# Gated linear attention and a maxout layer in one kernel: w2 by halves, weight loads interleaved, and a gate on the first token group

## The chip, the cores and the metric

The kernel runs on one core of one Trainium2 chip. The metric is the device time of one execution in microseconds. A core has TensorE (PE, matrix products), VectorE (DVE), ScalarE (ACT), GpSimd (POOL) and SyncE (SP), which here issues every DMA. Each engine works through its own list of instructions in order and waits for others on semaphores. Matmul results land in PSUM accumulators, which ScalarE or VectorE must empty.

## The reference

```python
B, H, S, D = 4, 8, 768, 48
for t in range(S):                       # attention with a decaying state
    state = alpha[:, :, t, :, None] * state + k[:, :, t] (outer) v[:, :, t]
    y[:, :, t] = q[:, :, t] @ state
x = y.transpose(0, 2, 1, 3).reshape(3072, 384)
out = maximum(x @ w1, x @ w2) @ w_out    # d_ff = 1024
```

All inputs and the output are fp32 in HBM: q, k, v and alpha 4.7 MB each, each weight 1.57 MB, the output 4.7 MB.

## The kernel before

**Attention in chunks.** The sequences are cut into 24 chunks of 128 tokens. Batch 0 is done in three double chunks of 256 tokens (functions d1, dcs, dexp, dqk, dtp, dp, dkv, dy; names with d), the other 18 chunks singly (a1, p1, a2, p2, p3, p4). A chunk takes the logarithm of alpha (ScalarE, dloga), sums it along time by matmuls with constant masks (TensorE, tile dcs or cs), makes exp of plus and minus the sum (ScalarE, den and dep), multiplies k and q by them (GpSimd dkt, VectorE dqt), transposes both (TensorE, dtp or tp), copies them out (dqk), forms the scores (TensorE, dpa and dpb), masks them (VectorE, dpt), and sums scores and the carried state into y (TensorE, dy or y). ScalarE copies y, transposed, into xT as fp16. The state passes from chunk to chunk through dkv, dw, dg, dt and dT.

**The maxout layer.** It uses max(x w1, x w2) = x w2 + relu(x (w1 - w2)). So wd = w1 - w2 is made once on VectorE in two halves (prep_wd, L657), M = w2 w_out is made once on TensorE, and the output is x M + relu(x wd) w_out. For M, w2 is cast to fp16 (copy, L653), transposed by 24 TensorE transposes (prep_t, L663, tile wtp), copied to w2T (prep_te), and multiplied with the cast w_out (prep_m, L677, tile mp; three blocks of 128 rows, each two calls of four matmuls). Tokens are then taken in groups of one to three chunks: eight h steps (fstep, L688, three matmuls each, as wide as the group) with a relu each (L693 on VectorE, L695 on ScalarE), and for each chunk an output tile in two halves (tstep: three matmuls with M at L702 and three of relu at L705; then five more at L705), a copy (outs) and a store (L715). h, y, mp and op share three PSUM accumulators.

**What sets the order.** A planner written in the kernel (Sched, L50) holds a list of operations with costs, dependencies and priorities, walks through them in planned time and emits each where the plan puts it. So the plan decides the order in each engine's list once, when the program is built; on the chip the engines follow that order whatever the real times are. The function refill (L939) adds token groups to the plan when TensorE would fall idle, from those chunks whose xT is planned to be done; a group takes fewer than three chunks only if TensorE would otherwise idle. The numbers in the op calls are planned costs.

**The opening.** All loads go through SP's one queue in this order: the first double chunk (alpha, k, q in two halves, and v), w2 whole (L221), w_out in two halves (L231), w1 in two halves (L221), the second and third double chunks (L201), then the single chunks (L192), whose buffers are slices of the weights' fp32 tiles, free once the casts and wd are done. Meanwhile the engines work through double chunk 0, the casts, the transposes, M, wd, and the first token groups.

```python
lw2 = prev = op("w2", 0, {"SP": WLOAD}, lambda e: load_w2(), ...)
for kind in ("wo", "w1"):
    for i in range(2):
        ...
w2c = [op("w2c", s, c, ... copy(e, w216[:, s, :], w2f[:, s, :]), deps=[lw2], prio=0.6) ...]
```

Of the kernel before, what the change touches and what calls it, by code (L numbers as in the profile page):

```python
# [49 lines left out]
class Sched:  # L50
# [49 lines left out]
    def run(self):  # L100
        while True:
            c = self.pick("PE")
            if c and self.refill:
                self.refill(c[1], c[1] > self.free["PE"] + 0.3)
            best = None
            for e in self.todo:
                c = self.pick(e)
                if c and (best is None or c[1] < best[0]):
                    best = (c[1], e, c[2])
            if best is None:  # L110
                if self.refill and self.refill(1e9, True):
# [24 lines left out]
def kernel(  # L136
# [27 lines left out]
    ND = NCH // 2  # L164
# [562 lines left out]
    def op(*a, **k):  # L727
        return Op(S, *a, **k)
# [41 lines left out]
    dloads_of(2, 0.6)  # L770

    w2c = [
        op("w2c", s, c, lambda e, s=s: copy(e, w216[:, s, :], w2f[:, s, :]), deps=[lw2], prio=0.6)
        for s, c in enumerate(({"ACT": 0.95}, {"DVE": 0.65}, {"ACT": 0.95, "DVE": 0.65}))
    ]
    wdc = [[op("wd", i, {"DVE": 1.7}, lambda e, i=i: prep_wd(i), deps=[lw1[i], lw2], prio=0.6)] for i in range(2)]
    woc = [op("woc", f, {"ACT": 0.75, "DVE": 0.55},
              lambda e, f=f: copy(e, wo16[:, f : f + 2, :], wof[:, f : f + 2, :]), deps=[lwo[f // 4]])
           for f in range(0, NF, 2)]
    for n in range(2 * ND, NCG):  # L780
        loads_of(n)
        if n == 2 * ND:
            G[n]["ld", 0].after.append(prev)
        if n < 2 * ND + 6:
            for i in range(4):
                G[n]["ld", i].deps.extend(woc if n < 2 * ND + 2 else w2c + wdc[0] + wdc[1])

    w2t = []
    for f in range(0, NF, 2):
        b = Buf(rx)  # L790
        t = op("w2t", f, {"PE": 0.4}, lambda e, f=f: prep_t(f), lat=0.17, deps=w2c, alloc=[b], prio=500 + f)
        w2t.append(op("w2te", f, {"DVE": 0.6, "ACT": 0.75}, lambda e, f=f: prep_te(e, f), deps=[t], reads=[b]))
    mdone = []
    prev = None
    for s in range(3):
        b = Buf(rm)
        for i in range(2):
# [7 lines left out]
    smask = op("mask", 0, {"DVE": 1.0}, lambda e: set_mask(), prio=0.1)  # L805
# [4 lines left out]
    rdloga, rdqt, rdkt, rdv, rdT, rdw, rdt32, rdgg, rdg = (Ring(2) for _ in range(9))  # L810
    B2 = []
    for m in range(ND):
        g = GD[m]
# [9 lines left out]

        def add(name, h, engs, fn, deps, lat=0.1, alloc=(), reads=(), **kw):
            o = GD[m - 1].get((name, h)) if m else None
            g[name, h] = op("d" + name, (m, h), engs, fn, lat=lat, deps=deps, after=[o, g.get((name, h - 1))],
                            alloc=[B[x] for x in alloc], reads=[B[x] if not isinstance(x, Buf) else x for x in reads],
                            prio=2 * m + 0.3 * h, **kw)
            return g[name, h]

        for h in range(2):
            al = lambda x: [x] if h == 0 else []
            re = lambda x: [x] if h else []
            add("a1", h, {"ACT": 0.43}, lambda e, m=m, h=h: d1(m, h), [g["ld", 0, h], sp1 if m == 1 else None],
                alloc=al("loga"), reads=[L[0]] + re("loga"))
            add("p1", h, {"PE": 0.5}, lambda e, m=m, h=h: dcs(m, h), [g["a1", h]], lat=0.17, alloc=[("cs", h)], reads=["loga"])
            add("en", h, {"ACT": 0.39}, lambda e, m=m, h=h: dexp(m, h, "en", -1.0), [g["p1", h]],
                alloc=al("en"), reads=[("cs", h)] + re("en"))
            add("ep", h, {"ACT": 0.39}, lambda e, m=m, h=h: dexp(m, h, "ep", 1.0), [g["en", h]],
                alloc=al("ep"), reads=[("cs", h)] + re("ep"))  # L840
            add("gg", h, {"ACT": 0.2}, lambda e, m=m, h=h: dgg(m, h), [g["ep", h]],
                alloc=al("gg"), reads=[("cs", h)] + re("gg"))
            add("kt", h, {"POOL": 1.0}, lambda e, m=m, h=h: dqk(m, h, 1), [g["en", h], g["ld", 1, h]],
                alloc=al("kt"), reads=["en", L[1]] + re("kt"))
            add("qt", h, {"DVE": 0.7}, lambda e, m=m, h=h: dqk(m, h, 2), [g["ep", h], g["ld", 2, h]],
                alloc=al("qt"), reads=["ep", L[2]] + re("qt"))
# [4 lines left out]
            add("v2", h, {"DVE": 0.64, "ACT": 0.92}, lambda e, m=m, h=h: dtpe(e, m, h), [g["p2", h]],  # L851
                alloc=[("qk", h)], reads=[("tp", h)])
            add("p3", h, {"PE": 0.36}, lambda e, m=m, h=h: dp(m, h), [g["v2", h]], lat=0.17,
                alloc=[("pa", h), ("pb", h)], reads=[("qk", h)], tiled=True)
            for t in range(2):
                add("m" + str(t), h, {"DVE": 0.62}, lambda e, m=m, h=h, t=t: dmask(m, h, t),
                    [g["p3", h], smask, g.get(("m0", h))],
                    alloc=[] if t else [("pt", h)], reads=[(("pa", "pb")[t], h)] + ([("pt", h)] if t else []))
        add("pk", 0, {"PE": 0.38}, lambda e, m=m: dkv(m), [g["kt", 1], g["v", 1]], lat=0.17,
# [26 lines left out]
    for n in range(2 * ND, NCG):  # L886
# [7 lines left out]

        def add(name, engs, fn, deps, lat=0.1, alloc=(), reads=(), **kw):

            g[name] = op(name, n, engs, fn, lat=lat, deps=deps, after=[dep(n - 1, name) if name != "a3" or n > 2 * ND else None],
                         alloc=[B[x] for x in alloc], reads=[B[x] if isinstance(x, str) else x for x in reads],
                         prio=n, **kw)
            return g[name]  # L900
# [4 lines left out]
        add("ep", {"ACT": 0.39}, lambda e, n=n: a2(n, "ep", 1.0), [g["en"]], alloc=["ep"], reads=["cs"])  # L905
        add("gg", {"ACT": 0.2}, lambda e, n=n: a2g(n), [g["ep"]], alloc=["gg"], reads=["cs"])
# [100 lines left out]
```

## Time and profile before

| what | value |
|---|---|
| five runs, median (lowest to highest) | 149.37 us (148.66 to 149.62) |
| the profiled execution: its time, its span | 148.21 us, 146.4 us |
| TensorE busy, matmuls | 131.2 us (90%), 1982 |
| ScalarE, VectorE, GpSimd busy | 98.5, 86.4, 81.4 us |
| granted TensorE clock | 0.999 |
| moved by DMA | 28.62 MB, 195 GB/s over the span |
| h matmuls by width | 48 of 128, 48 of 256, 144 of 384 columns |
| w1 - w2, two halves on VectorE | 1.76 us each, at 19.71 and 21.80 |
| M: first and last matmul start | 17.11 us, the last group of 18 at 18.91 for 3.10 |
| w2 lands | by 12.94 us (first cast) |
| last output copy | starts at 142.91 us |

Times in the page count from the span's start. A row of the trace holds a start, a duration, the engine, the line, the tile written and the tile read, the shape, a count of like instructions in a row, and in brackets the idle time ahead of it with what ended it. A matmul's bar contains a modelled end of some 0.2 us after its last column has gone in, so bars of matmuls that follow each other overlap.

### The profile page before, as it was taken

To read this page: it belongs to the slowest core of one execution; us is meant where nothing else is said; L and a number is where in the kernel's file an instruction comes from. 1 tells how busy PE (TensorE), PEld (TensorE's weight loads), DVE (VectorE), ACT (ScalarE), POOL (GpSimd) and SP (SyncE) were. 2 spreads that over 40 slices of the span, in tenths; PEclk is the share of its full clock that TensorE was granted. 3 is DMA by queue.
4 is the path that set the end of the run, shared out by engine and by line. 5 is a ranking of instruction groups with operands and counts; after the bars stand their busy time and mean duration, and the time that the engine had idled before them with its cause. 6 is when DMAs were issued, how large, how long until landed. Compare 5 with 4: busy or idle time off the path is not lost.

```text
span 146.4 us, 4919 instructions
## 1 busy us (share of the span) xinstructions
PE 131.2 (90%) x1982; PEld 87.2 (60%) x1982; DVE 86.4 (59%) x170; ACT 98.5 (67%) x221; POOL 81.4 (56%) x182
## 2 busy tenths in 40 slices
PE   0476995889999999999999999999999999999990
PEld 0354755576777666666656666566566666556550
DVE  4666657378797589547775788675749765000000
ACT  4437856498777687699767966597577854926721
POOL 7997001659988859757775958346859670000000
PEclk9999999999999999999999999999999999999999
DMA  4999999999987999998999979798997711113022
GB/s 123 263 381 380 380 333 263 236 251 203 211 167 174 206 187 245 209 221 189 236 192 220 260 173 235 140 267 193 225 240 158 166 58 54 54 43 116 7 80 81
DMA packets 93142, 28.62 MB, mean 195 GB/s; under 512 B 87872, under 2 KB 91968, under 8 KB 93120
## 3 DMA queue, kind: packets, MB, share of 16 engines
q1 hardware_dynamic: 93120, 28.32, 80.9%
q8 instruction: 15, 0.25, 0.7%
q14 instruction: 7, 0.06, 0.1%
HBM read 23.59 MB, written 4.72 MB: 193 GB/s over the span
## 4 chain that ended last, share of the span: by engine, by line
PE 63%; SPq 16%; DMA 9%; DVE 4%; ACT 3%; issue 2%; POOL 0%; ACTq 0%; DVEq 0%
PE op L705 20%; PE h L688 17%; PE op L702 7%; SPq L201 7%; DMA dqf<-in_q_dram 6%; PE y L463 5%; SPq L192 4%; SPq L221 3%; PE pa L404 3%; DMA w1f<-in_alpha_dram 3%; PE tp L386 2%; PE tp L388 2%; PE cs L328 2%; DVE dpt L559 2%; PE kv L415 2%
## 5 line engine op out<-in xcount | busy, mean ns | idle before, releaser
L705 PE MATMUL op<-wo,g 128*128 128x384 f16 x192 | 37.8, 326 | 0.0
L688 PE MATMUL h<-xT,wd 128*128 128x384 f16 (+2 forms) x240 | 37.3, 294 | 0.5 <-DVE g L693 0.4
L688 PEld LDWEIGHTS <-wd 128*128 128x128 f16 x240 | 20.1, 97 | 10.3 <-issue 0.8
L695 ACT ACTIVATE g<-h 128x384 f16<-128x384 f32 (+2 forms) x57 | 24.1, 443 | 3.1 <-PE h L688 2.8
L705 PEld LDWEIGHTS <-g 128*128 128x128 f16 x192 | 17.7, 97 | 10.9
L653 ACT COPY qk<-tp 128x1024 f16<-128x1024 f16 x14 | 14.2, 1012 | 4.1 <-PE tp L388 3.9
L653 ACT COPY outs<-op 128x384 f32<-128x384 f32 x16 | 7.7, 479 | 12.7 <-PE op L705 12.7
L365 POOL TENSOR_TENSOR T<-w,g 48x192 f16<-48x192 f32 x30 | 15.4, 512 | 1.1
L702 PE MATMUL op<-m,xT 128*128 128x384 f16 x72 | 15.7, 326 | 0.3 <-DVE g L693 0.3
L423 DVE TENSOR_TENSOR pt<-pa,u 128x512 f16<-128x512 f32 x18 | 12.4, 688 | 4.7 <-PE pb L404 4.3
L434 DVE TENSOR_TENSOR w<-kv,t 48x192 f32<-48x192 f32 x24 | 8.5, 354 | 9.3 <-PE kv L415 8.8
L519 POOL TENSOR_TENSOR dkt<-dkf,den 128x384 f16<-128x384 f32 x6 | 5.9, 995 | 13.0 <-ACT den L501 13.0
L693 DVE TENSOR_SCALAR g<-h 128x384 f16<-128x384 f32 (+2 forms) x23 | 9.8, 437 | 4.2 <-PE h L688 4.0
L423 DVE TENSOR_TENSOR pt<-pb,u 128x512 f16<-128x512 f32 x18 | 12.2, 680 | 0.0
L467 ACT CAST xT<-y 128x384 f16<-128x384 f32 x18 | 8.6, 480 | 5.0 <-PE y L463 4.8
L350 POOL TENSOR_TENSOR kt<-w2f,en 128x384 f16<-128x384 f32 x6 | 6.3, 1056 | 5.8 <-ACT en L338 3.7
L338 ACT ACTIVATE en<-cs 128x384 f32<-128x384 f32 x18 | 9.0, 498 | 0.8 <-PE cs L332 0.5
L463 PE MATMUL y<-pt,v 128*32 128x128 f16 x288 | 9.0, 220 | 0.0
L338 ACT ACTIVATE ep<-cs 128x384 f32<-128x384 f32 x18 | 8.9, 497 | 0.0
L702 PEld LDWEIGHTS <-xT 128*128 128x128 f16 x72 | 6.3, 97 | 4.0 <-issue 0.2
L350 POOL TENSOR_TENSOR kt<-w1f,en 128x384 f16<-128x384 f32 x6 | 6.2, 1032 | 4.2 <-issue 1.7
L486 PE MATMUL dcs<-dloga,c 128*128 128x192 f16 x6 | 1.6, 268 | 7.4 <-ACT dloga L476 7.4
(121 smaller groups left out, 276.1 us busy)
## 6 DMA issues: line engine op xcount, KB each, us to landing
out_dram<-outs SPq DMA_DIRECT2D x24, 192.0 KB, 3.2
w2f<-in_moe_w_dram SPq DMA_DIRECT2D x1, 1536.0 KB, 8.2
wof<-in_moe_w_out_dram SPq DMA_DIRECT2D x2, 768.0 KB, 9.8
w1f<-in_moe_w_dram SPq DMA_DIRECT2D x2, 768.0 KB, 12.2
dvf<-in_v_dram SPq DMA_DIRECT2D x3, 384.0 KB, 5.7
wof<-in_alpha_dram SPq DMA_DIRECT2D x6, 192.0 KB, 3.8
wof<-in_k_dram SPq DMA_DIRECT2D x6, 192.0 KB, 4.8
wof<-in_q_dram SPq DMA_DIRECT2D x6, 192.0 KB, 4.4
```

Source lines behind the costliest of these rows:

```text
L201: nc.sync.dma_start(out=dloads[m][i][:, hs], in_=src[0, hs, m * C2 : (m + 1) * C2, :].rearrange("h (p j) d -> p h (j d)", j=2),)
L338: nc.scalar.activation(out=t, in_=csv, func=ACTF.Exp, scale=scale)
L350: nc.gpsimd.tensor_mul(out=kts[n % NB][:, :, 0:D], in0=loads[n][1], in1=st[n]["en"])
L365: nc.gpsimd.tensor_mul(out=st[n]["T16"][ps, :, D * t : D * t + D], in0=st[n - 1]["w"][ps], in1=st[n]["g"][ps].unsqueeze(2).to_broadcast([D ...
L423: nc.vector.tensor_mul(out=s["pt"][:, t], in0=s["pp"][t], in1=ub)
L463: nc.tensor.matmul(y[o : o + 32, b // 4, :], lhsT=lhsT, rhs=rhs, start=start, stop=stop)
L653: {"ACT": nc.scalar.copy, "DVE": nc.vector.tensor_copy, "POOL": nc.gpsimd.tensor_copy}[e](out=out, in_=in_)
L688: nc.tensor.matmul(h[:, 0:W], lhsT=wd16[:, s, f * 128 : (f + 1) * 128], rhs=xT[:, s, a : a + W], start=(s == 0), stop=(s == 2))
L693: nc.vector.tensor_relu(gts[a][:, f, 0:W], hs[a, f][:, 0:W])
L695: nc.scalar.activation(out=gts[a][:, f, 0:W], in_=hs[a, f][:, 0:W], func=ACTF.Relu)
L702: nc.tensor.matmul(op, lhsT=xT[:, s, t0 : t0 + C], rhs=m16[:, s, :], start=(s == 0), stop=False)
L705: nc.tensor.matmul(op, lhsT=gts[a][:, f, i * C : (i + 1) * C], rhs=wo16[:, f, :], start=False, stop=(f == NF - 1))
```

## The change

- w2 is loaded as two halves of 512 columns; the weight loads follow each other as w2 half 0, w2 half 1, w_out half 0, w1 half 0, w_out half 1, w1 half 1 (before: w2, w_out twice, w1 twice).
- w2 is cast in six pieces of 128x512: row block 0 on ScalarE, 1 on VectorE, 2 on GpSimd, for each half; before, three pieces of 128x1024, two of them on ScalarE and one on VectorE as built.
- The transposes of w2 wait for their half alone, and a half sum of M for its two w2T copies and two casts of w_out alone; the priorities of these and of wd are raised.
- refill makes no token group until the first half of wd is planned to be done within 0.3 us.
- The planner prices TensorE at 1.9 times the cost before 19 us of planned time, some planned costs are altered, and ep and gg are planned to follow p1 (in order behind en), not to wait for en.
- In the built program the first token group has two chunks (24 h matmuls of 256 columns); before there were two groups of one (48 of 128). The other groups have the same widths. TensorE's list begins: double chunk 0 up to the transposes of its second half, 6 transposes of w2, scores, 18 transposes, dy, the 24 matmuls of M, both dcs of double chunk 1, 9 h, dtp, 9 h, dtp, 3 h. Before: all of double chunk 0, 24 transposes, M, 6 h, dcs, 3 h, dcs, 15 h, half an output tile, dtp, the other half, dtp.

```diff
+            if e == "PE" and t < 19.0:
+                cost *= 1.9
...
-    def load_w2():
-        load_w(moe_w2, w2f, slice(0, DFF))
+    def load_w2(i):
+        load_w(moe_w2, w2f, slice(i * FH, (i + 1) * FH))
...
+    def prep_w2(e, s, i):
+        c = slice(i * FH, (i + 1) * FH)
+        copy(e, w216[:, s, c], w2f[:, s, c])
...
-    dloads_of(0, 0.0)
-    lw2 = prev = op("w2", 0, {"SP": WLOAD}, lambda e: load_w2(), lat=1.6, after=[prev], prio=0.5)
-    lw1, lwo = [], []
-    for kind in ("wo", "w1"):
-        for i in range(2):
-            fn = {"wo": load_wo, "w1": load_w1}[kind]
-            prev = op(kind, i, {"SP": WLOAD / 2}, lambda e, i=i, fn=fn: fn(i), lat=1.6, after=[prev], prio=0.5)
-            (lwo if kind == "wo" else lw1).append(prev)
-    dloads_of(1, 0.3)
-    dloads_of(2, 0.6)
+    lw2, lw1, lwo = [None] * 2, [None] * 2, [None] * 2
+    for x in "d0 w20 w21 wo0 w10 wo1 w11 d1 d2".split():
+        if x[0] == "d":
+            dloads_of(int(x[1]), 0.3 * int(x[1]))
+        else:
+            i = int(x[2])
+            fn, to = {"w2": (load_w2, lw2), "wo": (load_wo, lwo), "w1": (load_w1, lw1)}[x[:2]]
+            prev = to[i] = op(x, i, {"SP": WLOAD / 2}, lambda e, i=i, fn=fn: fn(i), lat=1.6, after=[prev], prio=0.5)
...
+    w2c = [[op("w2c", (s, i), c, lambda e, s=s, i=i: prep_w2(e, s, i), deps=[lw2[i]], prio=-0.5)
+            for s, c in enumerate(({"ACT": 0.54}, {"DVE": 0.4}, {"POOL": 0.8}))] for i in range(2)]
+    wdc = [[op("wd", i, {"DVE": 1.7}, lambda e, i=i: prep_wd(i), deps=[lw1[i], lw2[i]], prio=0.2)] for i in range(2)]
...
-        t = op("w2t", f, {"PE": 0.4}, lambda e, f=f: prep_t(f), lat=0.17, deps=w2c, alloc=[b], prio=500 + f)
+        t = op("w2t", f, {"PE": 0.4}, lambda e, f=f: prep_t(f), lat=0.17, deps=w2c[f // NFH], alloc=[b], prio=f - 10)
...
-                      deps=w2t + woc[2 * i : 2 * i + 2], after=[prev], alloc=[b] if i == 0 else (), prio=800 + s)
+                      deps=w2t[2 * i : 2 * i + 2] + woc[2 * i : 2 * i + 2], after=[prev],
+                      alloc=[b] if i == 0 else (), reads=[b] if i else (), prio=0.4 + 0.01 * s)
...
+        if wdc[0][0].done is None or wdc[0][0].done > now + 0.3:
+            return
```

More of the change, by code (lines that the diff above doesn't have):

```diff
@@ L759, in dloads_of @@
                     GD[m]["ld", i, x] = prev
-    dloads_of(0, 0.0)
-    lw2 = prev = op("w2", 0, {"SP": WLOAD}, lambda e: load_w2(), lat=1.6, after=[prev], prio=0.5)
-    lw1, lwo = [], []
-    for kind in ("wo", "w1"):
-        for i in range(2):
-            fn = {"wo": load_wo, "w1": load_w1}[kind]
-            prev = op(kind, i, {"SP": WLOAD / 2}, lambda e, i=i, fn=fn: fn(i), lat=1.6, after=[prev], prio=0.5)
-            (lwo if kind == "wo" else lw1).append(prev)
-    dloads_of(1, 0.3)
-    dloads_of(2, 0.6)
[L772 to L776, printed above, removed]
+    lw2, lw1, lwo = [None] * 2, [None] * 2, [None] * 2
[9 more added lines that the diff above has]
+    wdc = [[op("wd", i, {"DVE": 1.7}, lambda e, i=i: prep_wd(i), deps=[lw1[i], lw2[i]], prio=0.2)] for i in range(2)]
     woc = [op("woc", f, {"ACT": 0.75, "DVE": 0.55},
-              lambda e, f=f: copy(e, wo16[:, f : f + 2, :], wof[:, f : f + 2, :]), deps=[lwo[f // 4]])
+              lambda e, f=f: copy(e, wo16[:, f : f + 2, :], wof[:, f : f + 2, :]), deps=[lwo[f // 4]], prio=-0.3)
            for f in range(0, NF, 2)]
@@ L785 @@
             for i in range(4):
-                G[n]["ld", i].deps.extend(woc if n < 2 * ND + 2 else w2c + wdc[0] + wdc[1])
+                G[n]["ld", i].deps.extend(woc if n < 2 * ND + 2 else w2c[0] + w2c[1] + wdc[0] + wdc[1])
     w2t = []
@@ L790 @@
         b = Buf(rx)
-        t = op("w2t", f, {"PE": 0.4}, lambda e, f=f: prep_t(f), lat=0.17, deps=w2c, alloc=[b], prio=500 + f)
-        w2t.append(op("w2te", f, {"DVE": 0.6, "ACT": 0.75}, lambda e, f=f: prep_te(e, f), deps=[t], reads=[b]))
+        t = op("w2t", f, {"PE": 0.4}, lambda e, f=f: prep_t(f), lat=0.17, deps=w2c[f // NFH], alloc=[b], prio=f - 10)
+        w2t.append(op("w2te", f, {"DVE": 0.6, "ACT": 0.75}, lambda e, f=f: prep_te(e, f), deps=[t], reads=[b], prio=-0.4))
     mdone = []
-    prev = None
     for s in range(3):
         b = Buf(rm)
+        prev = None
         for i in range(2):
             prev = op("m", s, {"PE": 0.66}, lambda e, s=s, i=i: prep_m(s, i), lat=0.17,
-                      deps=w2t + woc[2 * i : 2 * i + 2], after=[prev], alloc=[b] if i == 0 else (), prio=800 + s)
+                      deps=w2t[2 * i : 2 * i + 2] + woc[2 * i : 2 * i + 2], after=[prev],
+                      alloc=[b] if i == 0 else (), reads=[b] if i else (), prio=0.4 + 0.01 * s)
         mdone.append(op("mev", s, {"ACT": 0.4, "DVE": 0.45}, lambda e, s=s: copy(e, m16[:, s, :], mps[s]),
@@ L804 @@
     sp1 = op("pads", 1, {"DVE": 0.5}, lambda e: set_pads(1), prio=0.9)
-    smask = op("mask", 0, {"DVE": 1.0}, lambda e: set_mask(), prio=0.1)
+    smask = op("mask", 0, {"DVE": 1.5}, lambda e: set_mask(), prio=0.1)
     sdv = [op("dvT", i, {"POOL": 0.6}, lambda e, i=i: set_dvT(i), prio=(-1, 0.9)[i]) for i in range(2)]
@@ L810 @@
     rdloga, rdqt, rdkt, rdv, rdT, rdw, rdt32, rdgg, rdg = (Ring(2) for _ in range(9))
+    AFTER = {"ep": "en", "gg": "ep"}
     B2 = []
@@ L825, in add @@
             o = GD[m - 1].get((name, h)) if m else None
-            g[name, h] = op("d" + name, (m, h), engs, fn, lat=lat, deps=deps, after=[o, g.get((name, h - 1))],
+            g[name, h] = op("d" + name, (m, h), engs, fn, lat=lat, deps=deps, after=[o, g.get((name, h - 1)), g.get((AFTER.get(name), h))],
                             alloc=[B[x] for x in alloc], reads=[B[x] if not isinstance(x, Buf) else x for x in reads],
@@ L833 @@
             re = lambda x: [x] if h else []
-            add("a1", h, {"ACT": 0.43}, lambda e, m=m, h=h: d1(m, h), [g["ld", 0, h], sp1 if m == 1 else None],
+            add("a1", h, {"ACT": 0.45}, lambda e, m=m, h=h: d1(m, h), [g["ld", 0, h], sp1 if m == 1 else None],
                 alloc=al("loga"), reads=[L[0]] + re("loga"))
             add("p1", h, {"PE": 0.5}, lambda e, m=m, h=h: dcs(m, h), [g["a1", h]], lat=0.17, alloc=[("cs", h)], reads=["loga"])
-            add("en", h, {"ACT": 0.39}, lambda e, m=m, h=h: dexp(m, h, "en", -1.0), [g["p1", h]],
+            add("en", h, {"ACT": 0.44}, lambda e, m=m, h=h: dexp(m, h, "en", -1.0), [g["p1", h]],
                 alloc=al("en"), reads=[("cs", h)] + re("en"))
-            add("ep", h, {"ACT": 0.39}, lambda e, m=m, h=h: dexp(m, h, "ep", 1.0), [g["en", h]],
+            add("ep", h, {"ACT": 0.44}, lambda e, m=m, h=h: dexp(m, h, "ep", 1.0), [g["p1", h]],
                 alloc=al("ep"), reads=[("cs", h)] + re("ep"))
-            add("gg", h, {"ACT": 0.2}, lambda e, m=m, h=h: dgg(m, h), [g["ep", h]],
+            add("gg", h, {"ACT": 0.2}, lambda e, m=m, h=h: dgg(m, h), [g["p1", h]],
                 alloc=al("gg"), reads=[("cs", h)] + re("gg"))
-            add("kt", h, {"POOL": 1.0}, lambda e, m=m, h=h: dqk(m, h, 1), [g["en", h], g["ld", 1, h]],
+            add("kt", h, {"POOL": 1.05}, lambda e, m=m, h=h: dqk(m, h, 1), [g["en", h], g["ld", 1, h]],
                 alloc=al("kt"), reads=["en", L[1]] + re("kt"))
-            add("qt", h, {"DVE": 0.7}, lambda e, m=m, h=h: dqk(m, h, 2), [g["ep", h], g["ld", 2, h]],
+            add("qt", h, {"DVE": 0.9}, lambda e, m=m, h=h: dqk(m, h, 2), [g["ep", h], g["ld", 2, h]],
                 alloc=al("qt"), reads=["ep", L[2]] + re("qt"))
@@ L850 @@
                 alloc=[("tp", h)], reads=["qt", "kt"])
-            add("v2", h, {"DVE": 0.64, "ACT": 0.92}, lambda e, m=m, h=h: dtpe(e, m, h), [g["p2", h]],
+            add("v2", h, {"DVE": 0.66, "ACT": 0.95}, lambda e, m=m, h=h: dtpe(e, m, h), [g["p2", h]],
                 alloc=[("qk", h)], reads=[("tp", h)])
@@ L855 @@
             for t in range(2):
-                add("m" + str(t), h, {"DVE": 0.62}, lambda e, m=m, h=h, t=t: dmask(m, h, t),
+                add("m" + str(t), h, {"DVE": 0.66}, lambda e, m=m, h=h, t=t: dmask(m, h, t),
                     [g["p3", h], smask, g.get(("m0", h))],
@@ L895, in add @@
         def add(name, engs, fn, deps, lat=0.1, alloc=(), reads=(), **kw):
-            g[name] = op(name, n, engs, fn, lat=lat, deps=deps, after=[dep(n - 1, name) if name != "a3" or n > 2 * ND else None],
+            g[name] = op(name, n, engs, fn, lat=lat, deps=deps, after=[g.get(AFTER.get(name)), dep(n - 1, name) if name != "a3" or n > 2 * ND else None],
                          alloc=[B[x] for x in alloc], reads=[B[x] if isinstance(x, str) else x for x in reads],
@@ L904 @@
         add("en", {"ACT": 0.39}, lambda e, n=n: a2(n, "en", -1.0), [g["p1"]], alloc=["en"], reads=["cs"])
-        add("ep", {"ACT": 0.39}, lambda e, n=n: a2(n, "ep", 1.0), [g["en"]], alloc=["ep"], reads=["cs"])
-        add("gg", {"ACT": 0.2}, lambda e, n=n: a2g(n), [g["ep"]], alloc=["gg"], reads=["cs"])
+        add("ep", {"ACT": 0.39}, lambda e, n=n: a2(n, "ep", 1.0), [g["p1"]], alloc=["ep"], reads=["cs"])
+        add("gg", {"ACT": 0.2}, lambda e, n=n: a2g(n), [g["p1"]], alloc=["gg"], reads=["cs"])
         add("kt", {"POOL": 1.0}, lambda e, n=n: v1k(n), [g["en"], g["ld", 1]], alloc=["kt"], reads=["en", L[1]])
```

## The prediction

> **What bounds the kernel now.** I read the page's slices first, then the stretches of the opening, then the chain of waits there, then the rows of TensorE. The slices say where the time can go at all:
>
> ```profile
> PE   0476995889999999999999999999999999999990
> DMA  4999999999987999998999979798997711113022
> ```
>
> A slice is 3.66 us. From the tenth on TensorE is busy without a break, so from there the end is set by TensorE's own work; whatever another engine does is free unless it opens a hole. The holes are in the first 36 us, and DMA is full there. The stretches:
>
> ```profile
> 20.00:24.00 4.00, 2.48 (x21) 1.59 (x19) 3.67 (x4) 1.19 (x3) 0.00 (x0) 1.00 1.26 278
> 24.00:28.00 4.00, 3.26 (x43) 2.49 (x42) 2.03 (x8) 2.51 (x10) 2.27 (x4) 1.00 1.04 239
> 28.00:32.00 4.00, 3.63 (x89) 2.97 (x90) 2.48 (x6) 3.27 (x7) 2.38 (x5) 1.00 1.01 249
> ```
>
> (First PE busy, then the weight loads, VectorE, ScalarE, GpSimd.) The chain of waits names the two dates that pace this part:
>
> ```profile
> 17.99 9.10 DMA dqf<-in_q_dram
> ...
> 27.18 0.60 DVE dqt L517
> ...
> 27.82 0.62 PE dtp L531 x8
> ```
>
> The q of the second double chunk lands at 27.13, behind everything queued before it; its alpha lands at about 23.25 (dloga starts at 23.29). These two are DMA dates. The TensorE rows around them:
>
> ```profile
> 18.91 3.10 PE L677 MATMUL mp<-wo,w2T 128*128 128x384 f16 x18 [0.22 <-ACT w2T L653]
> 21.84 0.50 PE L688 MATMUL h<-xT,wd 128*128 128x128 f16 x6
> 23.86 0.24 PE L486 MATMUL dcs<-dloga,c 128*128 128x192 f16 x1 [1.52 <-ACT dloga L476]
> ...
> 24.89 1.24 PE L688 MATMUL h<-xT,wd 128*128 128x128 f16 x15
> 26.00 0.65 PE L702 MATMUL op<-m,xT 128*128 128x384 f16 x3
> 26.48 0.65 PE L705 MATMUL op<-wo,g 128*128 128x384 f16 x3
> 27.82 0.40 PE L531 MATMUL dtp<-ident,dqt 128*128 128x128 f16 x4 [0.69 <-DVE dqt L517]
> ```
>
> Reading these rows: a bar holds some 0.2 us of pipeline end, so I price by starts. 128x384 costs 0.1625 us (0.65 less the single bar 0.326, over two steps); 128x192 costs 0.083 (24.03 to 24.11); a group of eight transposes 0.46 (27.82 to 28.28). For the h matmuls two more rows:
>
> ```profile
> 29.98 0.68 PE L688 MATMUL h<-xT,wd 128*128 128x128 f16 x9
> 31.03 0.33 PE L688 MATMUL h<-xT,wd 128*128 128x128 f16 x3 [0.37 <-DVE g L693]
> ```
> ```profile
> 52.46 1.16 PE L688 MATMUL h<-xT,wd 128*128 128x256 f16 x9
> ```
>
> 128x128: (0.68 - 0.22) / 8 = 0.0575 us, a step of three 0.173. 128x256: (1.16 - 0.27) / 8 = 0.111, a step 0.333. The second line is a stall of another kind: the 128-wide step is shorter than its eviction on VectorE (0.28), there are three accumulators, and TensorE waits.
>
> **The change part by part.** *Wider first group (the gate).* The built order has one group of 256 tokens where there were two of 128: 24 h matmuls fewer. By the rows this saves 24 x (2 x 0.0575 - 0.111) = 0.1 us. The Trainium skill, "TensorE: Matmul & The Clock Gate", section "Back-to-back issue gap", puts 128 columns with a weight load each at about 81 ns sustained; by that the saving would be 24 x (0.162 - 0.111) = 1.2 us. The row is of this kernel and at full clock, so 0.1 us.
>
> *w2 in two halves.* 1.5 MB as two DMAs, one issue more on SP. Landings of half weights follow each other by about 2.1 us (w1 at 19.7 and about 21.8), so no fixed cost shows while the queue is full: 0 to 0.2 us (375 to 382 GB/s while halves flow against 400 while whole w2 does). I take 0.1, which moves alpha and q equally.
>
> *Casts of w2.* Six of 128x512 on ScalarE, VectorE and GpSimd for three of 128x1024. ScalarE gives up about 1 us. On GpSimd no such cast is shown; its 128x384 casts take 0.50 alone and 0.83 beside VectorE (the one at 9.42), so 0.67 to 1.1 each; I take 1.0, as VectorE works then. Queued behind them are dg, dt and the two dT, which dy waits for; but dy now stands behind all 24 transposes on TensorE. dT shifts from 13.65 to some 16 and dy from 13.1 to about 17.5: nothing.
>
> *wo and w1 interleaved.* Half 0 of w1 - w2 can be made at about 17.4 instead of 19.71, but the second half of wo lands at about 19.7 instead of some 17.3. The product w2 wo now does the half sums as they come: per column block four matmuls of half 0, then four of half 1. The first block's second half waits for the casts of wo (0.83), until about 20.5; then 20 matmuls x 0.1625 = 3.25, end 23.8 against 22.0. Those 1.8 us lie under the wait for alpha (dcs at 23.86) and cost about 0. Without that cover: 1.8 us. On ScalarE the third m cast now stands ahead of den, 24.0 to 24.4; den was at 24.47. Also 0. One condition: in the cold rows matmuls take twice as long (192 columns in 0.16 at 3.98); in the trace full speed is there by 17.1, after some 3.4 us without a gap. If it now comes at 20 or 21, the end moves by up to 1 us, and the wait for q takes that up.
>
> *The gate's price.* Before alpha and q land, the old order had filler: eight h steps (1.38) and the first half of an output tile (0.975), 2.36 in all. In the new order three 256-wide steps (1.0) stand ahead of the transposes that need q; no others could, since the relu of the first is queued on VectorE behind the multiply with q. Between dcs and 27.8 the new TensorE has 0.87 + 1.0 of work and idles about 2.0 us; the old idled 1.1. So at 27.82 the new one is 2.36 - 1.0 = 1.36 us of work behind. That is its cost if nothing gives it back.
>
> *What gives it back.* From 27.82 to dy at 35.98 I count the old order: 24 transposes 1.36, 16 matmuls of output 2.6, 24 h 1.38, two dcs sets 0.88, two dpa/dpb sets 0.69, dkv 0.25: 7.16 of 8.16 us, a hole of 1.0. It has three places: 30.5 to 31.03 (relu of a 128-wide step), about 0.2 at 33.0 (the same), the rest between pieces. The new order has five steps of 0.333 and both tokens' output tiles (3.6) between the same attention pieces, no 128-wide step, and the evictions (0.39 and 0.42 for 256) are as slow as a step. So I expect almost no hole: 1.0 back, dy again at 36. From 37.90 to 58.76 (the cs of the sixth single chunk) the same count (40 transposes 2.3, 28 output matmuls 4.55, 48 h of 128x256 5.3, five cs sets 1.35, 32 pa/pb 1.3 at 0.041, 72 y 1.4 at 0.019, dy 1.1, kv, dkv and dpa/dpb 1.2) gives 18.5 of 20.86 us: 2.4 us of holes, few of them visible, as the 0.2 us at each bar's end hides short ones. The visible ones are a wait for loga, whose alpha landed at 53.3, and for g at 57.3. With the DMA dates unchanged, a TensorE that is 0.4 us behind and has an output tile in hand where the old one had none meets fewer of them. Bounds: none goes (0 back) and all go (2.4). I take 1.4, a little over the middle: the waits for loads stay, those behind 128-wide relus have gone and the backlog is larger. After 59 there is backlog always: 0 to 0.2, and I take 0.1.
>
> Sum: +1.36 + 0.1 - 0.1 - 1.0 - 1.4 - 0.1 = about -1.15 us. On the profiled execution: 148.21 (span 146.4 and 1.8 around it) to 147.05. It lies 1.16 below the median of the five runs, 149.37; the same step from there gives 148.2.
>
> **The rivals.** *Nothing changes at the end.* The holes up to 59 are set by DMA (full until then), so TensorE reaches 59 with the same work done whatever it did at 25: the lost 1.36 comes back and no more. For it: DMA row 9 throughout, and wo, w1, d1 land in the same total time. That the gate and halves merely shuffle work under two DMA dates is the same case. 149.1 to 149.6, take 149.3.
>
> *Slower: the loss at 27.8 is not paid back.* TensorE's queue is in order; if it stands at the transposes for q for 2 us and again behind relus that queue after the q multiply on VectorE, the 1.36 remain, and the second half of w2 wo arriving later than the alpha adds up to 0.5. Against it are the 1.0 + 2.4 us of holes. It decides at holes after 27.82: over 3.3 us in the new trace it is slower. Price +1.3 to +1.9: about 150.9. The skill's same page, section "Why this matters for your kernels", warns of TensorE gaps over about 3 us, after which the clock halves; the new gap is 2.0, and after the old one of 1.52 dcs ran at 0.083, full speed. By the rule at 2.0 nothing happens; if it did, some 3 us of work would take double, to about 152.
>
> *The whole of it goes.* Eviction stalls and all other holes go up to 59: 147.0.
>
> **How the numbers follow.** About 0.5% (0.75 us) is what a measurement can tell from no change. The main case, 147.3 to 148.6, has 0.55; all holes gone (about 147.0) 0.12; nothing changes 0.18; slower 0.15. Of the main case nearly all is faster by over 0.5% (its edge, 148.6, is 0.77 below 149.37). So faster 0.67, same 0.18, slower 0.15. The range from 146.8 to 149.8 takes in the first three and leaves out most of the slower one.
>
> **What would show it.** Right: one group of 128x256 as the first h rows, no 128x128 h at all; w2 wo ends about 23.8; dcs within 0.3 of 23.9; dtp at 27.8 after a hole of about 2 us with nine h matmuls before it; dy of the second double chunk near 36.0; the sixth cs some 1 us earlier in work done; last op matmul near 141.7. Wrong: q landing later than 27.5 (then the order of loads costs), w2 wo still running at 25 (the clock or wo), holes of over 3 us between 28 and 59.

## The result, and the profile after

| | median | lowest to highest | runs | profiled execution: time, span | profiled a second time |
|---|---|---|---|---|---|
| before | 149.28 us | 147.33 to 150.87 | 79 | 148.21, 146.4 us | 149.91, 148.1 us |
| after | 147.86 us | 146.70 to 150.21 | 44 | 148.08, 146.3 us | 147.76, 146.0 us |

The ratio is 0.9933 (95% interval 0.9918 to 0.9949): 0.7% faster, which is 1.0 us; the medians in the table are 1.4 us apart. Ratios here and below take, of each kernel, only executions within 1.5% of its fastest, while medians take all; the second profile of before lies outside that band, at a granted clock of 1.00 like the other three.

The first two profiled executions hardly differ, because the one of before was a quick one (1.07 us under its median) and the one of after was 0.22 over. So each kernel was profiled once more, and both pairs are used below. The second one of before is 0.63 over its median: neither of its two profiles is its usual run, and the usual one lies between them.

The slices of the profile after:

```profile
PE   0465898799999979999999999999999999999990
DMA  4999999999989689999999999989899711103012
```

The second half is again without a break, here from the sixteenth slice (55 us) on; the opening is still uneven and DMA still full. The same stretches as before (time, PE, weight loads, VectorE, ScalarE, GpSimd), and then 48 to 60 us:

```profile
20.00:24.00 4.00, 3.96 (x22) 2.10 (x21) 1.89 (x2) 2.58 (x6) 0.00 (x0) 1.00 1.18 279
24.00:28.00 4.00, 2.80 (x37) 2.38 (x36) 1.55 (x4) 3.48 (x12) 2.32 (x3) 1.00 1.10 257
28.00:32.00 4.00, 4.00 (x80) 2.96 (x79) 3.22 (x8) 3.10 (x5) 3.01 (x8) 1.00 1.22 269
```
```profile
48.00:60.00 12.00, 10.93 (x183) 7.66 (x181) 8.52 (x18) 8.33 (x23) 8.23 (x19) 1.00 0.85 180
```

M (w2 times w_out) now fills 20 to 24, TensorE is emptier before 28, and it shows no gap from 28 to 32. The last row is the surprise of this execution: 1.07 us of visible gap at 48 to 60. The chain of waits names the load of q again, and then the alpha of the fifth single chunk, behind which that late gap lies:

```profile
17.90 8.62 DMA dqf<-in_q_dram
...
26.62 0.57 DVE dqt L519
...
27.24 0.62 PE dtp L533 x8
```
```profile
49.42 4.89 DMA w1f<-in_alpha_dram
```

The q landed at 26.52 (17.90 + 8.62), 0.6 us earlier than in the first profile of before (17.99 + 9.10 = 27.09), but just as in the second one of before (26.49). The rows of TensorE in the opening:

```profile
19.13 4.91 PE L683 MATMUL mp<-wo,w2T 128*128 128x384 f16 x24
24.43 0.24 PE L488 MATMUL dcs<-dloga,c 128*128 128x192 f16 x1 [0.39 <-ACT dloga L478]
...
25.29 1.14 PE L694 MATMUL h<-xT,wd 128*128 128x256 f16 x9
27.24 0.40 PE L533 MATMUL dtp<-ident,dqt 128*128 128x128 f16 x4 [0.81 <-DVE dqt L519]
```

No h matmul of 128 columns is left; M is done at 23.8 (its bar less the 0.2 us end); nine h matmuls stand ahead of the transposes, as foreseen. In the second profile of after the wait there is longer:

```profile
24.56 0.24 PE L488 MATMUL dcs<-dloga,c 128*128 128x192 f16 x1 [0.79 <-ACT dloga L478]
...
28.24 0.40 PE L533 MATMUL dtp<-ident,dqt 128*128 128x128 f16 x4 [1.67 <-DVE dqt L519]
```

**An account of the holes.** Bars hide short holes, so I count as the prediction did: the start of a marked matmul in the trace, less the work that TensorE's list puts ahead of it at start-to-start prices (0.1625, 0.111 and 0.0575 us for 384, 256 and 128 columns, and the prediction's other prices). What is left is all holes since the span's start; matmuls of the opening that ran slower than these prices are in it too. The list is known from the built program; its total work is 121.38 us before and 121.28 after. The cs matmuls of a chunk need the logarithm of its alpha, so their start shows whether TensorE had to wait for that load.

| holes so far, us | before | before, 2nd | after | after, 2nd |
|---|---|---|---|---|
| dy of double chunk 1 (35.98, 35.98, 35.67, 36.67) | 16.64 | 16.64 | 16.88 | 17.88 |
| cs of the 5th single chunk | 18.46 | 19.02 | 19.10 | 18.78 |
| cs of the 6th | 19.06 | 20.79 | 19.37 | 19.05 |
| cs of the 18th (last) | 20.94 | 22.67 | 21.03 | 20.71 |

Between the second profiles: +1.24 up to dy, -2.98 from there to the sixth cs, -0.22 after, and 0.10 less work: -2.06, where the spans differ by -2.1. Between the first: +0.24, +0.07, -0.22, -0.10: 0.0, where they differ by -0.1. So the change loses in the opening, and what it wins lies between dy and the sixth cs. Whether it wins there depends on the execution: between the fifth cs and the sixth the first profile of before lost 0.60 and the second 1.77; after lost 0.27 both times. That stretch gives 1.50 of the 2.98; the other 1.48 lies between dy and the fifth cs. Only the second profile of before shows this win, so the traces of the two kernels alone would not prove it; the experiments below have to.

The second profile of before shows how 1.77 comes about. Its chain of waits:

```profile
48.92 4.96 DMA w1f<-in_alpha_dram
...
53.96 0.52 ACT loga L323
54.48 0.07 ACT gg L342
54.55 0.56 ACT g L695 x2
55.10 0.12 SPq L715
55.23 0.04 issue
55.27 4.56 DMA w1f<-in_alpha_dram
...
59.91 0.53 ACT loga L323
```

The alpha of the fifth chunk takes 4.96 us (4.04 in the first profile). ScalarE has two relus queued behind its logarithm; by the chain a store on SP's queue is released after them, and behind that store stands the load of the sixth chunk's alpha, issued at 55.27 and not at 54.39. That load is slow too, 4.56 us against 3.7. TensorE then stands before the sixth cs:

```profile
60.49 0.32 PE L328 MATMUL cs<-loga,cmat 128*128 128x384 f16 x1 [0.96 <-ACT loga L323]
```

In after, TensorE lost 0.87 at the fifth cs, for a load of 4.89 us:

```profile
54.98 0.32 PE L330 MATMUL cs<-loga,cmat 128*128 128x384 f16 x1 [0.87 <-ACT loga L325]
```

But its sixth logarithm started without a wait at 58.78, one microsecond ahead of the matmul that needs it.

### The profile page after: what moved, and what is told of

It is laid out like the page before. It is cut to its first block, busy times and chain, and to the rows that moved or that the text cites. A ratio compares the mean times of both kernels' runs of the same rounds, so it can differ in the third digit from the quotient of the medians.

```text
span 146.3 us, 4865 instructions
## 1 busy us (share of the span) xinstructions
PE 131.4 (90%) x1958; PEld 87.7 (60%) x1958; DVE 83.2 (57%) x161; ACT 100.7 (69%) x223; POOL 82.6 (56%) x184
## 4 chain that ended last, share of the span: by engine, by line
PE 72%; SPq 12%; DMA 9%; ACT 2%; issue 1%; POOL 1%; DVE 0%; ACTq 0%; POOLq 0%; DVEq 0%
PE op L711 21%; PE h L694 20%; PE op L708 8%; SPq L203 7%; DMA dqf<-in_q_dram 6%; PE y L465 6%; DMA w1f<-in_alpha_dram 3%; SPq L223 3%; PE pa L406 3%; PE tp L388 3%; PE tp L390 2%; PE cs L330 2%; PE kv L417 2%; PE dtp L533 1%; SPq L233 1%
## 5 line engine op out<-in xcount | busy, mean ns | idle before, releaser
L711 PE MATMUL op<-wo,g 128*128 128x384 f16 x192 | 37.3, 326 | 0.0
L694 PE MATMUL h<-xT,wd 128*128 128x384 f16 (+1 forms) x216 | 36.6, 309 | 0.0
L701 ACT ACTIVATE g<-h 128x384 f16<-128x384 f32 (+1 forms) x53 | 23.7, 468 | 2.9 <-PE h L694 2.7
L694 PEld LDWEIGHTS <-wd 128*128 128x128 f16 x216 | 19.2, 98 | 9.2
L655 ACT COPY outs<-op 128x384 f32<-128x384 f32 x20 | 9.6, 479 | 14.9 <-PE op L711 14.9
L655 ACT COPY qk<-tp 128x1024 f16<-128x1024 f16 x15 | 15.2, 1014 | 2.5 <-PE tp L390 2.4
L367 POOL TENSOR_TENSOR T<-w,g 48x192 f16<-48x192 f32 x30 | 16.1, 536 | 1.2
L352 POOL TENSOR_TENSOR kt<-wof,en 128x384 f16<-128x384 f32 x6 | 6.5, 1086 | 8.6 <-ACT en L340 8.2
L699 DVE TENSOR_SCALAR g<-h 128x256 f16<-128x256 f32 (+1 forms) x19 | 8.6, 475 | 1.5 <-PE h L694 1.4
```

The source lines that it names most:

```text
L352: nc.gpsimd.tensor_mul(out=kts[n % NB][:, :, 0:D], in0=loads[n][1], in1=st[n]["en"])
L367: nc.gpsimd.tensor_mul(out=st[n]["T16"][ps, :, D * t : D * t + D], in0=st[n - 1]["w"][ps], in1=st[n]["g"][ps].unsqueeze(2).to_broadcast([D ...
L655: {"ACT": nc.scalar.copy, "DVE": nc.vector.tensor_copy, "POOL": nc.gpsimd.tensor_copy}[e](out=out, in_=in_)
L694: nc.tensor.matmul(h[:, 0:W], lhsT=wd16[:, s, f * 128 : (f + 1) * 128], rhs=xT[:, s, a : a + W], start=(s == 0), stop=(s == 2))
L701: nc.scalar.activation(out=gts[a][:, f, 0:W], in_=hs[a, f][:, 0:W], func=ACTF.Relu)
L711: nc.tensor.matmul(op, lhsT=gts[a][:, f, i * C : (i + 1) * C], rhs=wo16[:, f, :], start=False, stop=(f == NF - 1))
```

## The experiments

Besides the opening's edits, the diff alters the planner's book-keeping: some planned costs, and what ep and gg wait for in the plan. The prediction gave that no term. There are three theories. **A, the opening**: halves, interleaving and half sums give the gain. **W, the wide group**: it comes from the first group of 256 tokens and the vanished 128-wide steps, as the prediction argued. **O, the order**: it comes from the order that the planner writes after some 28 us, which the book-keeping shifts; the expectations of e1 to e4 call it theory B. Each ratio is against before, measured on the same chip.

| run | first groups, tokens | median, us | ratio [95%] |
|---|---|---|---|
| e1 | 256, 256 | 148.02 | 0.9928 [0.9890, 0.9966] |
| e2 | 256, 256 | 150.18 | 1.0101 [1.0030, 1.0172] |
| e3 | 256, 256 | 147.85 | 0.9961 [0.9927, 0.9995] |
| e4 | 256, 256 | 147.53 | 0.9900 [0.9852, 0.9947] |
| e5 | 128, 128 | 147.59 | 0.9899 [0.9860, 0.9938] |
| e6 | 256, 256 | 150.30 | 1.0074 [1.0039, 1.0108] |
| e7 | 256, 128 | 149.45 | 1.0031 [0.9994, 1.0069] |
| e8 | 128, 128 | 147.79 | 0.9915 [0.9877, 0.9952] |
| e11 | 256, 256 | 147.53 | 0.9880 [0.9844, 0.9916] |
| e12 | 256, 256 | 148.04 | 0.9929 [0.9890, 0.9968] |

**e1, the book-keeping alone.** Before, with only the book-keeping of the diff, of which a part is printed here; every load, cast and half sum stays as before.

```diff
+    AFTER = {"ep": "en", "gg": "ep"}
-            add("en", h, {"ACT": 0.39}, ... [g["p1", h]],
+            add("en", h, {"ACT": 0.44}, ... [g["p1", h]],
-            add("ep", h, {"ACT": 0.39}, ... [g["en", h]],
+            add("ep", h, {"ACT": 0.44}, ... [g["p1", h]],
...
-            add("qt", h, {"DVE": 0.7}, ...
+            add("qt", h, {"DVE": 0.9}, ...
...
-        add("ep", {"ACT": 0.39}, lambda e, n=n: a2(n, "ep", 1.0), [g["en"]], alloc=["ep"], reads=["cs"])
-        add("gg", {"ACT": 0.2}, lambda e, n=n: a2g(n), [g["ep"]], alloc=["gg"], reads=["cs"])
+        add("ep", {"ACT": 0.39}, lambda e, n=n: a2(n, "ep", 1.0), [g["p1"]], alloc=["ep"], reads=["cs"])
+        add("gg", {"ACT": 0.2}, lambda e, n=n: a2g(n), [g["p1"]], alloc=["gg"], reads=["cs"])
```

> The kernel before, with only the planner's book-keeping changed as in the change: ep and gg planned to follow p1 in order and not to wait for en, and the planned costs of the double chunks' operations and of the mask raised. Loads, casts, M and the gate are as before. Its plan also makes a first group of 256 tokens. Theory A (the opening's edits, halves, interleaving and half sums, give the gain): no change, 149.2. Theory B (the gain is the new order after 28 us, which the book-keeping alone brings about): -0.8 us, 148.4.

Measured 0.9928: the whole gain of the change, without one edit of the opening.

**e2, the change without the book-keeping.** After, with those lines put back.

```diff
-            add("ep", h, {"ACT": 0.44}, ... [g["p1", h]],
+            add("ep", h, {"ACT": 0.39}, ... [g["en", h]],
...
```

> The changed kernel, with that book-keeping put back (ep and gg wait for en again, the old planned costs), while halves, interleaved loads, six casts, half sums, gate and the 1.9 factor stay. Theory A: the gain stays, 148.0. Theory B: it goes, 149.2 to 149.7.

Measured 1.0101, more than either theory had put on it: all of the opening is there, and the kernel is slower than before. Theory A falls with e1 and e2 together. The stretch from 48 to 60 us in e2, with 1.34 us of visible gap:

```profile
48.00:60.00 12.00, 10.66 (x176) 6.86 (x172) 6.84 (x13) 8.53 (x20) 8.19 (x20) 1.00 0.95 194
```

**e3, the old load order.** TensorE's list stays that of after, word for word; on ScalarE and VectorE some casts and copies of the opening change places.

```diff
-    for x in "d0 w20 w21 wo0 w10 wo1 w11 d1 d2".split():
+    for x in "d0 w20 w21 wo0 wo1 w10 w11 d1 d2".split():
```

> The changed kernel with the weight loads in the old order (w2 halves, then both halves of w_out, then both of w1). TensorE's list is the same as after the change, so that only the interleaving is undone. Theory A: part of the gain goes, 148.4 to 149. Theory B: M is done about 1.8 us earlier and waits for alpha, nothing else moves: 147.9, as after the change.

**e4, w2 in one DMA.**

```diff
-        load_w(moe_w2, w2f, slice(i * FH, (i + 1) * FH))
+        if i == 0:
+            load_w(moe_w2, w2f, slice(0, DFF))
```

> The changed kernel with w2 loaded by one DMA, in the place of its first half; every list of instructions is otherwise the same. The casts of half 0 begin some 2 us later. Theory A: part of the gain goes, +0.3 to +0.8 us. Theory B: hidden before the waits for alpha and q at 23 to 27 us: 147.9, as after the change.

Measured 0.9961 and 0.9900, both about as fast as after (0.9933): the intervals overlap, so neither the interleaving nor the halves can be seen in the time (e3, at 0.9961, leaves room for a few tenths of a us). The stretch from 48 to 60 us of e3, and then of e4:

```profile
48.00:60.00 12.00, 12.00 (x200) 8.49 (x195) 9.42 (x20) 9.56 (x25) 9.96 (x20) 1.00 0.90 191
```
```profile
48.00:60.00 12.00, 12.00 (x193) 8.41 (x192) 9.58 (x21) 9.64 (x24) 9.92 (x21) 1.00 0.92 198
```

Where the order of after is kept, TensorE shows no gap here; the one in the first profile of after was that execution's late load.

**e5, e6: the two parts of the book-keeping.** Each is before with one part alone.

```diff
# e5: only what ep and gg wait for
+    AFTER = {"ep": "en", "gg": "ep"}
-            add("ep", h, {"ACT": 0.39}, ... [g["en", h]],
+            add("ep", h, {"ACT": 0.39}, ... [g["p1", h]],
...
# e6: only the planned costs
-            add("en", h, {"ACT": 0.39}, ...
+            add("en", h, {"ACT": 0.44}, ...
-            add("qt", h, {"DVE": 0.7}, ...
+            add("qt", h, {"DVE": 0.9}, ...
...
```

> The kernel before with one half of the book-keeping: ep and gg planned to follow p1, in order behind en, instead of waiting for en's planned end. Costs, loads, casts, M, no gate: as before. The plan keeps the two first groups of 128 tokens. Theory W (the wide first group brings the gain): no change, 149.0. Theory O (the order of the pieces brings it, whatever the width): laying the durations of the trace along the new lists gives -1.1, 148.0.

> The kernel before with the other half: the raised planned costs (double chunks, mask), with ep and gg waiting for en as before. The plan now makes a first group of 256 tokens. Theory W: -0.8 to -1.1, 148.0. Theory O: the durations along this list give +1.3, 150.3, in spite of the wide group.

Measured 0.9899 for e5, which keeps both groups of 128 tokens, and 1.0074 for e6, whose first group has 256. Theory W falls: the width goes against the time in both. The waits of TensorE in e6 from 36 to 62 us, in total, times, and longest:

```profile
PE cs L328 <- ACT loga L323: 1.4, 1, 1.4
...
PE h L688 <- ACT xT L646: 0.6, 1, 0.6
...
PE h L688 <- ACT g L695: 0.2, 1, 0.2
```

**e7, the gate alone**, in before.

```diff
+        if wdc[0][0].done is None or wdc[0][0].done > now + 0.3:
+            return
```

> The kernel before with the gate alone (no token group until the first half of w1 - w2 is planned to be done). Groups of 256, 128, 384 and so on. Theory W: faster, 148 to 148.5. Theory O: +0.7, 149.8.

Measured 1.0031, about +0.5 us: no gain, as theory O had it (+0.7). The gate alone turns the first two groups into one of 256 and one of 128 tokens. In the changed kernel it does nothing: the built lists of all five engines are the same with and without it. There the other edits already delay the first group.

**e8, a change that means nothing.** The planner counts an attention step on TensorE as ready a margin later than its inputs, and puts maxout work first if that is ready earlier. Here the margin is 0.01 us larger.

```diff
-    MARGIN = 0.25
+    MARGIN = 0.26
```

> The kernel before with one number of the planner changed, MARGIN 0.25 to 0.26, which nudges the order on TensorE and nothing else; the groups keep their widths (128, 128, 256, ...). Theory W: no change. Theory O: the durations along its list give -1.1, 148.0: as much as the whole change, from a nudge.

Measured 0.9915: as much as the whole change. All five lists are those of before until about 55 us of planned time: on TensorE up to the first h step behind the fifth cs, on VectorE up to a relu at the same place, on the others some 5 us longer. From the fifth cs to the sixth, as built (pa and pb in pairs):

```
before: cs, 3 h, 4 kv, 8 tp, 3 h, 28 y, 3 h, 4 pa/pb, 6 op, 8 tp,             cs
e8:     cs, 6 h, 8 tp, 4 kv, 28 y, 3 h, 6 op, 4 pa/pb, 8 tp, 5 op, 4 kv,      cs
```

Ahead of the sixth cs e8 puts five output matmuls and a kv more, 0.99 us of work. Its trace there:

```profile
57.44 0.65 PE L705 MATMUL op<-wo,g 128*128 128x384 f16 x3
...
58.81 0.98 PE L705 MATMUL op<-wo,g 128*128 128x384 f16 x5
59.62 0.33 PE L415 MATMUL kv<-v,kt 128*128 128x96 f16 x4
59.79 0.33 PE L328 MATMUL cs<-loga,cmat 128*128 128x384 f16 x1
```

The five matmuls at 58.81 lie where TensorE waits in the second profile of before, and the cs follows without a wait: 0.22 us of holes between the two cs, against 0.60 and 1.77. From there to the last cs e8 has 1.77, before 1.88. So what its list gains against either profile of before is gained at this one place; up to the fifth cs the lists are the same, and what differs there (holes of 18.9 us against 18.5 and 19.0) is the spread of executions. In this execution the loads were not late: the sixth logarithm had started at 57.91, before the five matmuls. So the trace shows that the spare work stands there, not yet that it covers a late load.

e5 bears it out: by the fifth cs its list holds the same work as before's, in another order, and between the fifth and the sixth cs it has five output matmuls more, 0.81 us. The order in SP's queue does not go with the time: e5, e8 and e11 are faster with the store still directly ahead of the sixth alpha, and e2 and e6 are slower with that alpha ahead of the store.

**e9, e10: both kernels once more**, unchanged, for a second profile of each.

> The kernel before once more, for a second profile: its first one is 1.1 us below the median. Theory O: the extra time of the usual execution lies in further holes of TensorE between 24 and 60 us; from 60 on about 1.9 us of holes as in the first profile. Theory A: in a longer opening (first dcs later than 23.9).

> The changed kernel once more, for a second profile. Theory O: without the late landing at 54.4 of the first profile the holes from the first to the sixth cs are about 1.2 us, as in the runs with the old load order and with w2 whole, in place of 2.5.

They gave the table of holes. Theory O's forecast for both came true: e9's further holes lie between dy and the sixth cs, 1.88 follow, and e10 has 1.17 in place of 2.49. What theory A asked for is in e9 as well, a first dcs at 24.16 in place of 23.86, behind an M that ended at about 22.4, 0.6 us later; but the transposes of q started at 27.82 in both, so this cost nothing. Their date is the end of the multiply with q. That the two dates are equal is chance: in e9 the q landed 0.6 us earlier, and the multiply took 1.20 us in place of 0.60.

```profile
18.33 8.16 DMA dqf<-in_q_dram
...
26.58 1.20 DVE dqt L517
...
27.82 0.62 PE dtp L531 x8
```

**e11, e12: other orders.** e11 is before with e5's edit and four planner constants altered, and none of the opening's edits. e12 is after with w2 whole and three constants altered.

```diff
# e11
-    SEM = 0.06
-    MARGIN = 0.25
+    SEM = 0.1
+    MARGIN = 0.3
-    LOAD, WLOAD = 1.06, 3.9
+    LOAD, WLOAD = 1.08, 3.9
-            G[n]["ld", i] = op("ld", n, ... lat=3.1, ...
+            G[n]["ld", i] = op("ld", n, ... lat=3.4, ...
...
# e12
-    MARGIN = 0.25
+    MARGIN = 0.3
-    LOAD, WLOAD = 1.06, 3.9
+    LOAD, WLOAD = 1.08, 3.9
-            G[n]["ld", i] = op("ld", n, ... lat=3.1, ...
+            G[n]["ld", i] = op("ld", n, ... lat=3.2, ...
```

> The kernel before with ep and gg planned behind p1 (as in the deps run) and four planning numbers changed (SEM 0.10, MARGIN 0.30, planned cost of a single chunk's load 1.08 and its latency 3.4): nothing of the opening's edits. Theory O: the durations of the trace along this order give -1.9 against the kernel before, 147.3, below the changed kernel. Theory A: 149.

> The changed kernel with w2 loaded whole and three planning numbers changed (MARGIN 0.30, load cost 1.08, latency 3.2). Theory O: -1.9 against the kernel before, 147.3, equal to the run without the opening's edits. If the opening's edits are worth something of their own beside the order, this one is faster than that one.

Measured 0.9880 and 0.9929, 1.8 and 1.1 us less than before where 1.9 was expected of both: e12 missed. e11 has the lowest ratio of all, without the opening's edits. Its interval, 0.9844 to 0.9916, ends just under that of after, 0.9918 to 0.9949; they come from different sets of executions, so that e11 beats after is likely and not shown. e12 adds nothing to after.

**What tells the orders apart.** For each built list, TensorE's work ahead of the sixth cs, added up afterwards at the same prices:

| list | work ahead, us | ratio |
|---|---|---|
| e6 | 37.76 | 1.0074 |
| e2 | 38.40 | 1.0101 |
| e7 | 38.58 | 1.0031 |
| before | 39.70 | 1 |
| after, e3, e4 | 40.42 | 0.9933, 0.9961, 0.9900 |
| e5 | 40.51 | 0.9899 |
| e8 | 40.69 | 0.9915 |
| e11 | 40.84 | 0.9880 |
| e12, e1 | 42.36, 42.43 | 0.9929, 0.9928 |

All lists with 40.4 or more are faster, none with 39.7 or less is, and beyond 40.8 more work brings nothing. The sixth logarithm starts at 57.9 to 59.9 in the profiles of before, after and e8, and each list has to have other work until then. The holes up to the sixth cs go with it: 20.3 to 21.4 us in the profiles of e2, e6 and e7, 18.3 to 19.4 in those of all faster lists, 19.06 and 20.79 in those of before. But it is a count made afterwards, over lists that lose their time in different places (e7 most of it before the third cs, e6 before the fourth). e8 is the one run in which nothing is changed ahead of the fifth cs.

## Why the prediction was right, and where it was not

The time was right: 148.2 forecast, 147.86 measured; -1.15 against -1.42 between the medians, or -1.0 by the ratio. The cause that it gave was not, and so the hit was luck in its largest term: the prediction had no term for the book-keeping, which brings the whole gain by itself (e1), and without which the rest of the change is slower than before (e2).

- *Wider group, 24 h fewer, -0.1*: as built, and too small to be seen alone. The row's price stands, not the 81 ns of the Trainium skill ("TensorE: Matmul & The Clock Gate", section "Back-to-back issue gap"): the second profile of before has six such matmuls in 0.50 us, (0.50 - 0.22) / 5 = 0.056 each:

```profile
22.45 0.50 PE L688 MATMUL h<-xT,wd 128*128 128x128 f16 x6
```

- *w2 in halves, +0.1*: the logarithm of alpha starts at 23.85, 23.99, 24.02 and 24.16 in the four profiles with halves (after twice, e2, e3), and from 23.29 to 24.52, mean 23.8, in the ten with w2 whole. About +0.2, within the spread.
- *Casts*: 0.86 and 0.85 us on GpSimd, inside the bounds of 0.67 to 1.1; hidden, as expected. dy of double chunk 0 started at 17.70 (17.5).
- *wo and w1 interleaved, 0*: M ended at 23.8 (23.8) and dcs began at 24.43 and 24.56 (23.9, within 0.3: missed, by 0.2 and 0.4). The alpha came later than in the first profile of before, and dcs waited for it by 0.39 and 0.79. The condition on the clock came true in part: in the first profile of after the first matmuls of M lie 0.3 us apart (19.13 to 19.74) and not 0.1625, and full speed is there by 20.8. No cost of the interleaving can be seen in e3's time.
- *The price at q, +1.36*: the lists put 12.18 and 10.82 us ahead of those transposes, exactly 1.36 apart. By starts (nine h are 1.0 us) the hole was 0.95 in the first profile and 1.81 in the second (2.0). But to call it the gate's price was wrong: the gate is without effect in this kernel.
- *Back by dy, -1.0*: mis-sized. From the transposes to dy, after needed 8.43 us for 7.97 of work in both profiles, a hole of 0.46 and not about none: 0.54 came back. At dy the changed kernel was 0.24 or 1.24 behind, where 0.36 was forecast; the 1.0 between its two profiles is when the first multiply with q ended, 27.19 or 28.20 (why is told in the last section).
- *From dy to the sixth cs, -1.4*: the step that failed in its reason, and the largest gain of the sum. The prediction took 1.4 as a little over the middle between nothing and 2.4, because 128-wide relus had gone and an output tile was in hand. Measured there: +0.07 in the first profiles and -2.98 in the second. It is 1.17 us of holes in the second profile of after (forecast 1.0), and 4.15 in that of before, where the forecast had only seen the 2.4 of a quick execution. e5 and e8 gain as much with the 128-wide steps in place, and e6 loses with the wide group: the wide group was not the reason. An output tile in hand was right in kind, but it is the planner's order that puts it there: five matmuls in e5 and in e8.
- *After it, -0.1*: -0.22. The last op matmul starts at about 142.5 and 142.2 in the two profiles of after, not near 141.7: that figure was worked from the quick execution of before.
- *Rivals*: "nothing changes" is right that DMA dates rule the opening (e9's later M moved nothing), and wrong that they rule up to 59: there a list with more work ahead of the next load uses the time. "Slower" had its price, 1.24 behind at dy in one of two profiles, and failed at its point: it asked for over 3.3 us of holes after q, and after had 0.46 + 2.49 and 0.46 + 1.17 up to the sixth cs. Other orders do reach it: e6 has 3.87 between the first cs and the sixth, and it is slower.

What stays open: between before and after the order differs in many places, and which swap makes after faster was not isolated; only for e8 is it known to within a few steps. That spare work ahead of the sixth cs covers late loads fits the count and the holes, but no run delays a load to try it. Whether e5 or e11 beats after is open too.

## What to carry to other kernels

When a planner writes the order, any edit of its costs reshuffles all that follows: before crediting the edit, run the same kernel with a meaningless change of one planning constant (here 0.01 us gave -0.85%) and with each half of the diff alone. Where loads set dates, ask of an in-order engine how much work its list holds ahead of the matmul that needs the next load; here, with 0.7 to 1.1 us more of it, the time was 0.4 to 1.2% less (after, e3, e4, e5, e8, e11). And where executions spread by more than the effect, profile twice: between two executions of before the account of holes differed by 1.7 us.

## What the runs showed of the hardware

- A load of 192 KB, issued at about the same time in the same program (49.27 and 48.92), took 4.04 and 4.96 us (alpha of the fifth chunk, two executions of before), and 4.89 once in after. The 0.57 us by which its logarithm was late (53.39, 53.96) grew to 1.74 at the next one (58.17, 59.91): 0.88 through the later issue of the next alpha behind a store in the same queue (54.39, 55.27), and about 0.86 because that load took 4.56 us and not 3.7.
- VectorE's multiply with q and GpSimd's multiply with k, each one instruction of 128x384, overlap in both executions of after, and one of the two is slow. In the first it is GpSimd's (two multiplies in 2.36 us):

```profile
26.62 0.56 DVE L519 TENSOR_TENSOR dqt<-dqf,dep 128x384 f16<-128x384 f32 x1 [2.45 <-DMA dqf<-in_q_dram]
```
```profile
25.68 2.36 POOL L521 TENSOR_TENSOR dkt<-dkf,den 128x384 f16<-128x384 f32 x2 [9.76 <-ACT den L503]
```

In the second profile of after it is VectorE's:

```profile
26.83 1.36 DVE L519 TENSOR_TENSOR dqt<-dqf,dep 128x384 f16<-128x384 f32 x1 [2.47 <-DMA dqf<-in_q_dram]
```
```profile
25.82 1.96 POOL L521 TENSOR_TENSOR dkt<-dkf,den 128x384 f16<-128x384 f32 x2 [10.16 <-ACT den L503]
```

In these executions the one that starts first keeps its time. In the first execution VectorE starts at 26.62 and GpSimd's second multiply at 26.64: 0.56 and 1.40 us. In the second GpSimd starts at 26.77 and VectorE at 26.83: 1.00 and 1.36. In the second profile of before GpSimd starts at 26.36 and VectorE at 26.58: 0.99 and 1.19. In its first GpSimd was done at 27.04, VectorE started at 27.18, and neither lost anything (0.99 and 0.60). So a few hundredths of a us in the landing of q decide which engine loses 0.4 to 0.8 us, and this made up 0.8 of the 1.0 us between the two starts of the q transposes in after (27.24 and 28.24); the other 0.2 is the landing itself (26.52, 26.73).
